# When the second MLP's weights are converted: two scopes of a one-core kernel cut 28 slots earlier, and the conversion's share of each slot set anew

## The chip, the core and the metric

One core of one Trainium2 chip runs the whole program. The metric is the device time of one launch in microseconds, as the median of three runs; a profiled execution of the same kernel has a time and a span of its own, given below.

## What is computed

Attention through 32 landmarks with a Newton inverse, then two mixers with an MLP behind each. All arrays are float32.

```python
B, H, S, D = 8, 8, 576, 64
x = (A @ Z @ C @ v)                                  # attention, then (B, S, 512)
h = x^T @ U @ V;  u = x + h^T                        # first mixer, rank 32
x = u + relu(u @ w_ch1) @ w_ch2                      # first MLP, 512 -> 2048 -> 512
mixed = real(fft(fft(x, axis=1), axis=2))            # second mixer
u = x + mixed
un = (u - mean(u)) / sqrt(var(u) + 1e-6)
out = u + relu(un @ w2_ch1) @ w2_ch2                 # second MLP
```

## The kernel before

**Numbers and weights.** Each float32 operand of a large product is split into a high and a low part, and three TensorE products stand for one. The weights come as 64-bit words. They are converted on the chip, once, into high and low parts of one tile of 128x1024 words: 512 KB come in, 512 KB go out to a scratch array `staged` (names `d` in the profile), from which the MLP loads them later. Such a conversion of one tile is a *staging*.

**Passes and slots.** Each MLP is run as two passes of 1024 hidden columns each: pass 0 and pass 1 of the first MLP, 2 and 3 of the second. A pass goes over chunks of 512 tokens (9 chunks in passes 0 and 1, 3 in passes 2 and 3). `Mlp.stream(p)` is a generator that a hand-written loop steps: one step is a *slot*, twelve 128x512 products on TensorE. A chunk is 16 slots: 8 that go up (L238 to L240, drained by a relu on ScalarE at L242 and a subtraction on VectorE at L243) and 8 that go down (L291 to L293, added at L302). The up products go through three PSUM banks in turn. Pass 0 takes chunk 0 in two halves, the second half last. At the end of a pass the weights of the next one are loaded (`w<-d` in the profile, L194), and residues and inputs of the next chunk are loaded beside them (L157, L146). All these transfers and those of the staging are issued by SyncE (SP) in the order of the code.

**Beside pass 0.** The attention of batch b runs in slots of the same loop (`slots.add`, `Batch.steps`); it ends, with the tail of the last batch, in slot 118 of 147 of that loop. The 16 tiles of pass 1 are staged there by `staging` (one generator step in every third slot, two in the others), 10 steps for a tile. Then the attention's pools are given back.

**Beside passes 1 to 3.** A second scope opens pools for the Fourier mixers. Mixer b (`Mixer.steps`) is spread over some 30 slots from `starts[b]`: folds, products over channels and tokens, unfolding, and the norm (`centre`, `sum_sq`, `sums_low` at L1250, `deviation`, whose product at L1255 waits for `sums_low`). The 32 tiles of passes 2 and 3 are staged by `staging_pairs`, and after them 28 sums of blocks of these weights by `staging_sums`. Both are one generator with prices, and `Pace.step(us)` lets it spend `us` in a slot: a tile costs 1.1 + 1.1 + 1.4 = 3.6. `room(s)` gives the slot's allowance. A tile has four parts: the split of the tile before it (ScalarE L50 and GpSimd L51 into the one buffer `stg`, which has to be stored before it is written again), then three pairs of VectorE instructions (L1379 with L1380; L1386 with L1388, and an absolute value on ScalarE at L1387; L1390 with L1391). What `Pace` has not done when the loop ends is done by `later.rest()` in one go.

**The last part.** `Mlp.pairs` runs the remaining six chunks of passes 2 and 3 as pairs by a seven-product scheme (L329 to L331). Its `prepare` loads normalised inputs (`acc<-un`, L146), splits them (ScalarE L389, VectorE L376), and its products start from banks that ScalarE copies (L406).

Of the kernel before, what the change touches and what calls it, by code (L numbers as in the profile page):

```python
# [28 lines left out]
HM = FF // P // 2  # L29
# [11 lines left out]
def body(ctx: ExitStack, tc: tile.TileContext, qT, kT, vn, mU, mV, w11, w12, w21, w22,  # L41
# [68 lines left out]
    def stage(cv, src, dst, bufs, raw=None):  # L110
        if raw is None:
            raw = cv.tile([P, 1024], U32, name="wraw", bufs=2)
        fetch_raw(raw, src)
        yield from wait(5)
        st = cv.tile([P, 2, 512], F32R, name="stg", bufs=1)
        yield from convert(cv, raw, st, bufs)
        yield from wait(1)
        nc.sync.dma_start(dst, f32(st))
# [1198 lines left out]
    def pool(name, **k):  # L1317
        return tc.tile_pool(name=name, bufs=1, reuse_waits="tile", **k)

    def chained(gens):  # L1320
        for g in gens:
            yield from g

    def some(gen, n):
        for _ in range(n):
            next(gen, 0)
# [21 lines left out]
    passes = [(U1, U1, ByChunk(y1), None), (U1, ByChunk(y1), X1, staged[1]),  # L1348
              (UN, None, ByChunk(y2), staged[2]), (UN, ByChunk(y2), ByChunk(y3), staged[3])]

    def staging(cv, p, bufs=1):
        return chained([stage(cv, srcs[p][i], staged[p][i], bufs) for i in range(2 * HM)])

    def staging_pairs(cv, passes):
        tiles = [(srcs[p][i], staged[p][i]) for p in passes for i in range(2 * HM)]
        raws = []

        def fetch():
            if len(raws) < len(tiles):
                raw = cv.tile([P, 1024], U32, name="wraw", bufs=2)  # L1360
                fetch_raw(raw, tiles[len(raws)][0])
                raws.append(raw)
                due["raw"] = clock[0] + 2

        fetch()
        former = None
        for i, (_, dst) in enumerate(tiles):
            yield from ready("raw")
            u = raws[i].rearrange("p (n two) -> p n two", two=2)
            lo, hi = u[:, :, 0], u[:, :, 1]  # L1370
            if former:
                st = cv.tile([P, 2, 512], F32R, name="stg", bufs=1)
                split(st[:, 0, :], st[:, 1, :], former[0], nc.gpsimd)
            fetch()
            yield 1.1
            a = cv.tile([P, 512], U32, name="cva", bufs=2)
            p = cv.tile([P, 512], U32, name="cvp", bufs=1)
            pf, af = f32(p), f32(a)
            nc.vector.tensor_scalar(a, hi, 3, 0x3FFFFFFF, op0=ALU.logical_shift_left, op1=ALU.bitwise_and)  # L1379
            nc.vector.scalar_tensor_tensor(out=a, in0=hi, scalar=0xC0000000, in1=a, op0=ALU.bitwise_and,  # L1380
                                           op1=ALU.bitwise_or)
            yield 0
            if former:
                nc.sync.dma_start(former[1], f32(st))
            yield 1.1
            nc.vector.tensor_scalar(p, a, 0xFF800000, None, op0=ALU.bitwise_and)  # L1386
            nc.scalar.activation(f32(hi), f32(hi), AF.Abs)  # L1387
            nc.vector.scalar_tensor_tensor(out=pf, in0=lo, scalar=2.0 ** -52, in1=pf, op0=ALU.mult, op1=ALU.mult)  # L1388
            yield 1.4
            nc.vector.tensor_tensor(pf, pf, af, op=ALU.add)  # L1390
            nc.vector.scalar_tensor_tensor(out=af, in0=f32(hi), scalar=MINNORM, in1=pf, op0=ALU.is_ge, op1=ALU.mult)  # L1391
            former = af, dst
            yield 0
        st = cv.tile([P, 2, 512], F32R, name="stg", bufs=1)
        split(st[:, 0, :], st[:, 1, :], former[0], nc.gpsimd)
        yield 0
        nc.sync.dma_start(former[1], f32(st))
# [85 lines left out]
    with pool("mm") as mp, pool("pm", space=PSUM) as pm:  # L1483
# [31 lines left out]
                old = new  # L1515
            yield from old

        EARLY = 8
        with pool("aa") as ap_, pool("ac") as ac, pool("cv0") as cv0, pool("pt", space=PSUM) as psb:
            t = {}  # L1520
            batches = [Batch(ap_, psb, t, b, mlp) for b in range(B)]
            slots = Slots()
            FIRST, GAP = -1 - Batch.LAST, 11
            half = (0, 1, 2, 4, 6, 8, 9, 10)
            for b in range(B):
                slots.add(GAP + STEPS * (b - 1) - 23 + 2 * (b == 1) if b else FIRST, batches[b].steps(batches[b + 1] if b + 1 < B else None))
            slots.add(GAP + STEPS * (B - 1) - 10, [(0, lambda: mlp.get_tail(B))])
            slots.add(GAP + STEPS * (B - 1) - 8, ((k, lambda k=k: mlp.hand_tail(B, k)) for k in range(4)))

            slots.add(FIRST, [(11, lambda: place_v(t))])  # L1530

            sums = {**{n - 11: [(1, 'k', 3 * n, 3 * n + 3)] for n in range(6)}, 3: [(2, 'k', 0, 6)], 5: [(2, 'k', 6, 12)], 7: [(2, 'k', 12, 18)]}

            def filler(s):

                if s in sums:
                    for b, nm, first, last in sums[s]:
                        batches[b].landmark_sums(nm, first, last)
                    return

                ps = mlp.bank()
                for _ in range(6):
                    nc.tensor.matmul(ps[:, 0:P], t["ident"], t["ident"], start=True, stop=True)

            with tc.manual_schedule():
                for what in "kq":
                    batches[0].load(what)
                attention_constants(ac, t)
                small, large = attention_setup(t, ap_, cv0), direct()
                some(small, 1)  # L1550
                some(large, 1)
                batches[0].load("v")
                some(large, 1)
                convs = chained([small, large])
                for s in range(FIRST, 0):
                    slots.run(s)
                    if s - FIRST in (6, *range(10, 20)):
                        filler(s)
                    some(convs, 0 if s < FIRST + 4 else 1 + s % 2)
                later, gen = staging(cv0, 1, 2), mlp.stream(0)  # L1560
                for s in range(N + GAP - 8):
                    if s >= GAP or s in half:
                        next(gen)
                    else:
                        filler(s)
                    slots.run(s)
                    if s < GAP + 13:
                        some(convs, 2)
                        if s == GAP + 12:
                            some(convs, 99)  # L1570
                    else:
                        some(later, 1 if s % 3 == 2 else 2)
                some(later, 999)
                some(gen, 9)
        with tc.manual_schedule():
            scales = Scales(rs)
            mlp.plan(UN, [(c, c + 1) for c in range(PLAIN, NCH, 2)], quarters)
            with pool("cv") as cv, pool("fp") as fp, pool("fc") as fc, pool("pf", space=PSUM) as psb:
                f = {}
                slots = Slots()  # L1580
                starts = (33, 58, 83, 108, 133, 157, 182, 206)
                for b, s in enumerate(starts):
                    slots.add(s, Mixer(fp, psb, f, b).steps(b + 1 == B))
                later = Pace(chained([staging_pairs(cv, (2, 3)), staging_sums(cv)]))
                gen = mlp.stream(1)
                setup = fourier_setup(f, fc, fp)

                def room(s):
                    r = s - max((a for a in starts if a <= s), default=-99)
                    return 1.45 if r > 40 else 1.4 if r in (*range(10, 21), 23, 24) else .7 if r in (4, 9, 21, 22) else 0  # L1590

                for s in range(N + 2 * PLAIN * STEPS - LEAD):
                    if s in (N, N + PLAIN * STEPS):
                        some(gen, 9)
                        gen = mlp.stream(2 + (s > N))
                    next(gen)
                    slots.run(s)
                    next(setup, 0)
                    later.step(room(s))
                later.rest()  # L1600
            assert not slots.at
            with pool("tl") as mlp.last_pool, pool("tp", space=PSUM) as mlp.last_ps:
                last = mlp.pairs(quarters, Y, scales, U2, ByChunk(y3))
                next(last)
                for s in range(LEAD):
                    next(gen)
                    next(last)
                    next(last)
                some(gen, 9)
                for _ in last:  # L1610
                    pass
# [83 lines left out]
```

## Time and profile before

| | us |
|---|---|
| median of 3 runs | 1787.58 (1785.87 to 1788.69) |
| the profiled execution | 1789.14 |
| its span in the profile | 1787.4 |
| TensorE busy in it | 1757.6 (98%) |
| VectorE busy | 1171.2 (66%) |
| ScalarE busy | 735.6 (41%) |
| GpSimd busy | 328.2 (18%) |

The span is what the trace covers; 1.7 us of the execution lie around it. In this trace pass 0's loop reaches slot 119 at about 495 us, pass 1 begins at 571, mixer 0's first slot is at 661, and the pairs begin at about 1305.

### The profile page before, as it was taken

Reading aid. Unit: us, or ns where it says so; the run is one execution under the profiler, and the core shown is the slowest. Engines: PE = TensorE matmul, PEld = TensorE weight load, DVE = VectorE, ACT = ScalarE, POOL = GpSimd, SP = SyncE. Lnnn points to the kernel's source line nnn. Section 1 sums busy time; section 2 is a strip of 40 time slices with the busy share of each in tenths; the row PEclk is TensorE's granted clock in tenths of the full one; section 3 lists DMA queues with packets and bytes.
Section 4 is the critical chain, followed back from the end, with each engine's and each line's share of the span. In section 5 each row is a group of like instructions: output and inputs, shape, how many; then the busy total and the mean of one; then the engine's idle time right before and its main releaser. Section 6 shows DMA issues by size and latency. Waiting matters only on the chain.

```text
span 1787.4 us, 30912 instructions
## 1 busy us (share of the span) xinstructions
PE 1757.6 (98%) x11905; PEld 1432.7 (80%) x11905; DVE 1171.2 (66%) x2028; ACT 735.6 (41%) x1520; POOL 328.2 (18%) x314
## 2 busy tenths in 40 slices
PE   6999999999999999999999999999999999999999
PEld 4777777777788888888878888888878888888887
DVE  7897666566322977888886665657575674577564
ACT  4554443444211333433342333434256445454642
POOL 3324211221110321211111122211111001100100
PEclk9999999999999999999999999999999999999999
DMA  7555456443536764546555954776688778878764
GB/s 254 182 174 171 152 175 206 155 162 105 179 137 249 242 234 154 183 164 216 179 179 193 329 200 148 273 281 201 222 290 273 216 243 257 261 228 247 223 214 153
DMA packets 215895, 371.00 MB, mean 208 GB/s; under 512 B 28970, under 2 KB 129930, under 8 KB 215748
## 3 DMA queue, kind: packets, MB, share of 16 engines
q1 hardware_dynamic: 211140, 359.59, 60.9%
q10 hardware_dynamic: 4608, 9.44, 1.4%
q8 instruction: 94, 1.54, 0.4%
q14 instruction: 53, 0.43, 0.1%
HBM read 262.18 MB, written 106.17 MB: 206 GB/s over the span
## 4 chain that ended last, share of the span: by engine, by line
PE 88%; DVE 7%; DMA 2%; ACT 1%; issue 1%; SPq 0%; POOL 0%; DVEq 0%; ACTq 0%
PE ps L291 9%; PE ps L293 9%; PE ps L292 9%; PE ps L238 9%; PE ps L240 8%; PE ps L239 8%; PE ps L329 7%; PE ps L331 7%; PE ps L330 7%; PE ps L554 1%; PE ps L553 1%; PE ps L555 1%; PE ps_f L77 1%; PE ps_f L76 1%; PE ps_f L75 1%
## 5 line engine op out<-in xcount | busy, mean ns | idle before, releaser
L238 PE MATMUL ps<-x,w 128*128 128x512 f32 x768 | 305.4, 398 | 0.2 <-DVE g L243 0.2
L291 PE MATMUL ps<-g,w 128*128 128x512 f32 x768 | 304.2, 396 | 0.0
L240 PE MATMUL ps<-x,w 128*128 128x512 f32 x768 | 299.8, 390 | 0.0
L293 PE MATMUL ps<-g,w 128*128 128x512 f32 x768 | 299.8, 390 | 0.0
L239 PE MATMUL ps<-x,w 128*128 128x512 f32 x768 | 299.4, 390 | 0.0
L292 PE MATMUL ps<-g,w 128*128 128x512 f32 x768 | 299.2, 390 | 0.0
L243 DVE SCALAR_TENSOR_TENSOR g<-ps,g 128x512 fp32r<-128x512 f32 x192 | 132.4, 690 | 206.7 <-ACT g L242 206.4
L242 ACT ACTIVATE g<-ps 128x512 fp32r<-128x512 f32 x192 | 114.0, 597 | 264.0 <-PE ps L240 263.4
L291 PEld LDWEIGHTS ps<-g,w 128*128 128x128 f32 x768 | 144.3, 188 | 31.9 <-issue 3.5
L240 PEld LDWEIGHTS ps<-x,w 128*128 128x128 f32 x768 | 144.1, 188 | 31.4
L293 PEld LDWEIGHTS ps<-g,w 128*128 128x128 f32 x768 | 144.1, 188 | 31.1
L238 PEld LDWEIGHTS ps<-x,w 128*128 128x128 f32 x768 | 144.3, 188 | 29.9 <-DVE g L243 0.6
L292 PEld LDWEIGHTS ps<-g,w 128*128 128x128 f32 x768 | 144.4, 188 | 27.4
L239 PEld LDWEIGHTS ps<-x,w 128*128 128x128 f32 x768 | 144.4, 188 | 26.9
L302 DVE TENSOR_TENSOR xf<-ps,xf 128x512 f32<-128x512 f32 x88 | 60.5, 687 | 86.7 <-PE ps L293 84.6
L406 ACT COPY ps<-ps 128x512 f32<-128x512 f32 x126 | 72.4, 575 | 94.4 <-PE ps L331 93.4
L51 POOL TENSOR_TENSOR stg<-cva,stg 128x512 fp32r<-128x512 f32 x48 | 65.4, 1363 | 216.8 <-ACT stg L50 190.4
L458 POOL TENSOR_TENSOR w<-w,w 128x512 f32<-128x512 f32 x24 | 33.3, 1389 | 362.1 <-DMA w<-rs 181.6
L329 PE MATMUL ps<-xs,w 128*128 128x512 f32 x240 | 94.2, 392 | 1.9 <-ACT ps L406 1.9
L331 PE MATMUL ps<-xs,w 128*128 128x512 f32 x240 | 94.1, 392 | 0.0
L330 PE MATMUL ps<-xs,w 128*128 128x512 f32 x240 | 93.9, 391 | 0.0
L51 POOL TENSOR_TENSOR x<-xf,x 128x512 fp32r<-128x512 f32 (+7 forms) x48 | 60.1, 1254 | 157.9 <-ACT x L50 122.7
(420 smaller groups left out, 3356.9 us busy)
## 6 DMA issues: line engine op xcount, KB each, us to landing
w<-e SPq DMA_DIRECT2D x84, 512.0 KB
w<-d SPq DMA_DIRECT2D x126, 256.0 KB
w<-d SPq DMA_DIRECT2D x60, 512.0 KB
wraw<-w SPq DMA_DIRECT2D x56, 512.0 KB
d<-stg SPq DMA_DIRECT2D x48, 512.0 KB
y<-xf SPq DMA_DIRECT2D x64, 256.0 KB
xf<-y SPq DMA_DIRECT2D x52, 256.0 KB
u<-u1T ACTq DMA_DIRECT2D x32, 288.0 KB
```

The lines of the kernel that those rows point to most:

```text
L51: (eng or nc.vector).tensor_tensor(lo, src, f32(hi), op=ALU.subtract)
L238: nc.tensor.matmul(ps, wh, xh, start=k == 0, stop=False)
L239: nc.tensor.matmul(ps, wl, xh, start=False, stop=False)
L240: nc.tensor.matmul(ps, wh, xl, start=False, stop=k == 3)
L242: nc.scalar.activation(g[:, 0, :], ps, AF.Relu)
L243: nc.vector.scalar_tensor_tensor(out=g[:, 1, :], in0=ps, scalar=0.0, in1=f32(g[:, 0, :]), op0=ALU.max, op1=ALU.subtract)
L291: nc.tensor.matmul(ps, wh, gh, start=k == m0, stop=False)
L292: nc.tensor.matmul(ps, wl, gh, start=False, stop=False)
L293: nc.tensor.matmul(ps, wh, gl, start=False, stop=k == m1 - 1)
L329: nc.tensor.matmul(ps, wh, xh, start=first and k == 0, stop=False, skip_group_check=True)
L330: nc.tensor.matmul(ps, wl, xh, start=False, stop=False, skip_group_check=True)
L331: nc.tensor.matmul(ps, wh, xl, start=False, stop=last and k == 1, skip_group_check=True)
```

## The change

The first scope ends with slot `end`, the last slot that holds a step of the attention plus one: 119, where it was 147. (The change's own words count 27 slots; the loop counts 28, slots 119 to 146.) `staging` stages 14 of the 16 tiles of pass 1. The two others go into `staging_pairs`, ahead of the 32 tiles of passes 2 and 3, and this generator starts in slot 119 of pass 0, in the new pools, with an allowance of 1.6 a slot. In pass 1 the allowance ahead of mixer 0 is 1.6 where it was 1.45; beside the mixers it stays 1.4 in 13 slots of each (r = 10 to 20, 23, 24), and the .7 in r = 4, 9, 21 and 22 is gone.

```diff
-    def staging(cv, p, bufs=1):
-        return chained([stage(cv, srcs[p][i], staged[p][i], bufs) for i in range(2 * HM)])
+    def staging(cv, n):
+        return chained([stage(cv, srcs[1][i], staged[1][i], 2) for i in range(n)])
-    def staging_pairs(cv, passes):
-        tiles = [(srcs[p][i], staged[p][i]) for p in passes for i in range(2 * HM)]
+    def staging_pairs(cv, first):
+        tiles = [(srcs[p][i], staged[p][i]) for p in range(1, 4) for i in range(2 * HM)][first:]
...
-        EARLY = 8
+        EARLY, ALONG = 8, 14
...
-                later, gen = staging(cv0, 1, 2), mlp.stream(0)
-                for s in range(N + GAP - 8):
+                later, gen = staging(cv0, ALONG), mlp.stream(0)
+                end = max(slots.at) + 1
+                for s in range(end):
...
                 some(later, 999)
-                some(gen, 9)
+                assert not slots.at
...
             with pool("cv") as cv, pool("fp") as fp, pool("fc") as fc, pool("pf", space=PSUM) as psb:
+                later = Pace(chained([staging_pairs(cv, ALONG), staging_sums(cv)]))
+                for s in range(end, N + GAP - 8):
+                    next(gen)
+                    later.step(1.6)
+                some(gen, 9)
...
-                later = Pace(chained([staging_pairs(cv, (2, 3)), staging_sums(cv)]))
...
-                    return 1.45 if r > 40 else 1.4 if r in (*range(10, 21), 23, 24) else .7 if r in (4, 9, 21, 22) else 0
+                    return 1.6 if r > 40 else 1.4 if r in (*range(10, 21), 23, 24) else 0
```

TensorE's products stand in the same order before and after. Three places show what moves on the others.

On SP, at the end of pass 0 (stores of `y` are the second half of chunk 0, `w<-d` are weights of pass 1, `wraw<-w` fetches a tile to be staged, `d<-stg` stores one). Before:

```order
L160 DMA y_0_75<-xf 128x512
L194 DMA w_6945<-d_8_114 128x1024
L194 DMA w_6947<-d_9_115 128x1024
L160 DMA y_0_75<-xf 128x512
L194 DMA w_6970<-d_10_116 128x1024
L194 DMA w_6972<-d_11_117 128x1024
L160 DMA y_0_75<-xf 128x512
```

and of the change:

```order
L160 DMA y_0_75<-xf 128x512
L194 DMA w_7082<-d_8_114 128x1024
L194 DMA w_7084<-d_9_115 128x1024
L87 DMA wraw<-w 128x1024
L160 DMA y_0_75<-xf 128x512
L194 DMA w_7116<-d_10_116 128x1024
L194 DMA w_7118<-d_11_117 128x1024
L1384 DMA d_7_129<-stg 128x1024
L160 DMA y_0_75<-xf 128x512
```

A fetch and a store of 512 KB have come between the weights that pass 1 loads.

On VectorE, in the norm of mixer 0, ahead of the subtraction into `le` on which L1255 waits. Before:

```order
L1390 TENSOR_TENSOR cvp<-cvp,cva 128x512
L1391 SCALAR_TENSOR_TENSOR cva<-wraw,cvp 128x512
L51 TENSOR_TENSOR x<-xf,x 128x512
L1250 TENSOR_TENSOR ho<-cc,ho 128x288
L1379 TENSOR_SCALAR cva<-wraw 128x512
L1380 SCALAR_TENSOR_TENSOR cva<-wraw,cva 128x512
L302 TENSOR_TENSOR xf<-ps,xf 128x512
L1265 TENSOR_TENSOR Z<-U,ps_l 128x1152
L1386 TENSOR_SCALAR cvp<-cva 128x512
L1388 SCALAR_TENSOR_TENSOR cvp<-wraw,cvp 128x512
L51 TENSOR_TENSOR x<-xf,x 128x512
```

and of the change:

```order
L51 TENSOR_TENSOR x<-xf,x 128x512
L1250 TENSOR_TENSOR ho<-cc,ho 128x288
L1379 TENSOR_SCALAR cva<-wraw 128x512
L1380 SCALAR_TENSOR_TENSOR cva<-wraw,cva 128x512
L302 TENSOR_TENSOR xf<-ps,xf 128x512
L1265 TENSOR_TENSOR Z<-U,ps_l 128x1152
L1386 TENSOR_SCALAR cvp<-cva 128x512
L1388 SCALAR_TENSOR_TENSOR cvp<-wraw,cvp 128x512
L1390 TENSOR_TENSOR cvp<-cvp,cva 128x512
L1391 SCALAR_TENSOR_TENSOR cva<-wraw,cvp 128x512
L51 TENSOR_TENSOR x<-xf,x 128x512
```

The pair L1390 and L1391 has gone from the front of this stretch to its end; the count of staging instructions in it is the same six.

On SP, at the entry of the pairs, ahead of the first `acc<-un` (`rs<-r` stores the last mixer's scale, `e` are sums of blocks). Before:

```order
L1293 DMA rs_205<-r 128x288
L1441 DMA e_2_180<-cva 128x512
L1441 DMA e_2_180<-wraw 128x512
L1441 DMA e_1_179<-stg 128x512 x2
L1441 DMA e_3_181<-cva 128x512
L1441 DMA e_3_181<-blk 128x512
L146 DMA acc<-un_193 128x256
```

and of the change:

```order
L192 DMA w_13722<-d_0_122 128x2x256
L192 DMA w_13722<-d_1_123 128x2x256
L1293 DMA rs_205<-r 128x288
L146 DMA acc<-un_193 128x256
L146 DMA acc<-un_194 128x256
```

The six stores of the last sums no longer stand between the last mixer and the loads of the pairs.

## Rows read from the trace of the kernel before

**Rows 1.** The page: its span, and each engine's busy time and instructions.

```profile
span 1787.4 us, 30912 instructions
...
PE 1757.6 (98%) x11905; PEld 1432.7 (80%) x11905; DVE 1171.2 (66%) x2028; ACT 735.6 (41%) x1520; POOL 328.2 (18%) x314
```

**Rows 2.** TensorE's waits from 495 us to the end.

```profile
PE ps_l L1255 <- DVE le L1250: 2.7, 3, 1.4
PE ps L329 <- ACT ps L406: 1.9, 1, 1.9
PE ps_f L1202 <- DVE Z L51: 0.6, 1, 0.6
PE ps L238 <- DVE g L243: 0.2, 1, 0.2
```

**Rows 3.** TensorE's timeline at the entry of the pairs: start, length, instruction.

```profile
1321.31 0.50 PE L329 MATMUL ps<-xs,w 128*128 128x512 f32 x1 [1.88 <-ACT ps L406]
...
1322.58 0.61 PE L331 MATMUL ps<-xs,w 128*128 128x512 f32 x1
...
1325.97 0.41 PE L330 MATMUL ps<-xs,w 128*128 128x512 f32 x1
```

**Rows 4.** ScalarE's timeline at the same place.

```profile
1309.56 0.62 ACT L50 CAST cva<-blk 128x512 fp32r<-128x512 f32 x1 [4.33 <-DMA e<-cva]
...
1320.16 0.62 ACT L389 CAST xs<-acc 128x512 fp32r<-128x512 f32 x1 [1.83 <-DMA acc<-un]
1320.68 1.06 ACT L406 COPY ps<-ps 128x512 f32<-128x512 f32 x2
```

**Rows 5.** SP's timeline of issues at the same place.

```profile
1304.92 0.60 SPq L1293 DMA_DIRECT2D rs<-r  x1
...
1311.98 3.73 SPq L146 DMA_DIRECT2D acc<-un  x8
```

**Rows 6.** Stretches: us, busy PE, PEld, DVE, ACT, POOL, clock, DMA share, GB/s.

```profile
549.00:571.00 22.00, 22.00 (x99) 18.22 (x98) 7.31 (x11) 4.46 (x8) 2.63 (x2) 1.00 0.86 299
571.00:593.00 22.00, 22.00 (x99) 18.22 (x98) 14.75 (x23) 8.22 (x14) 2.87 (x3) 1.00 1.00 358
593.00:661.00 68.00, 68.00 (x302) 56.31 (x301) 59.13 (x82) 23.04 (x41) 23.59 (x20) 1.00 0.61 212
1319.00:1326.00 7.00, 5.12 (x16) 3.74 (x16) 5.50 (x9) 5.38 (x11) 0.00 (x0) 0.76 1.04 376
```

**Rows 7.** VectorE's groups by line, 571 to 661 us: busy, mean ns, idle before.

```profile
L1380 DVE SCALAR_TENSOR_TENSOR cva<-wraw,cva 128x512 uint32<-128x512 uint32 x13 | 11.9, 918 | 0.4
L243 DVE SCALAR_TENSOR_TENSOR g<-ps,g 128x512 fp32r<-128x512 f32 x16 | 11.0, 688 | 11.6 <-ACT g L242 11.6
L1386 DVE TENSOR_SCALAR cvp<-cva 128x512 uint32<-128x512 uint32 x12 | 10.5, 872 | 0.1
L1390 DVE TENSOR_TENSOR cvp<-cvp,cva 128x512 f32<-128x512 f32 x12 | 9.3, 779 | 0.2
L1388 DVE SCALAR_TENSOR_TENSOR cvp<-wraw,cvp 128x512 f32<-128x512 uint32 x12 | 8.4, 701 | 0.4
L1391 DVE SCALAR_TENSOR_TENSOR cva<-wraw,cvp 128x512 f32<-128x512 f32 x12 | 8.3, 692 | 1.4 <-DVE cvp L1390 0.5
L1379 DVE TENSOR_SCALAR cva<-wraw 128x512 uint32<-128x512 uint32 x13 | 7.5, 574 | 0.0
```

**Rows 8.** ScalarE's longest wait, 571 to 661 us: total, times, longest.

```profile
ACT stg L50 <- DMA d<-stg: 24.7, 9, 5.1
```

**Rows 9.** VectorE's timeline in pass 1 ahead of the mixers.

```profile
624.26 0.42 DVE L1379 TENSOR_SCALAR cva<-wraw 128x512 uint32<-128x512 uint32 x1
...
629.43 0.69 DVE L243 SCALAR_TENSOR_TENSOR g<-ps,g 128x512 fp32r<-128x512 f32 x1 [4.02 <-ACT g L242]
```

**Rows 10.** VectorE's timeline in the norm of mixer 0.

```profile
740.39 1.52 DVE L1379 TENSOR_SCALAR cva<-wraw 128x512 uint32<-128x512 uint32 x1
...
750.09 0.88 DVE L1250 TENSOR_TENSOR le<-cc,le 128x288 fp32r<-128x288 f32 x1
```

**Rows 11.** GpSimd's timeline there.

```profile
740.28 1.35 POOL L51 TENSOR_TENSOR stg<-cva,stg 128x512 fp32r<-128x512 f32 x1 [8.67 <-ACT stg L50]
```

## The prediction

> **What bounds the kernel now.** I read the page first: TensorE is busy 98% of the span, 1757.6 of 1787.4 us [rows 1], and the change leaves its products and their order alone. So only its idle time and its clock can move. TensorE's waits come next, from the place where the change begins (495 us) to the end: they are few, 1.9 + 2.7 + 0.6 + 0.2 = 5.4 us [rows 2]. Earlier waits lie in the attention's start, which is the same in both kernels up to slot 100 or so. The reader should see two kinds. The norm's product L1255 waits three times for VectorE, 2.7 us, the longest 1.4 [rows 2]: in mixers 0 and 2, beside conversions, and a little in mixer 7. And the first product of the pairs that needs a copied bank waits 1.88 us for ScalarE's L406 [rows 3]. Behind that wait the clock is low: the granted share from 1319 to 1326 us is 0.76 [rows 6], and from 1322.58 to 1325.97 eight products start 0.42 us apart, 3.39 us in all [rows 3], where at full rate 68 us hold some 300, 0.227 each [rows 6], or twelve to a slot of 2.72. That is 3.39 - 8 x 0.227 = 1.6 us more at 1.2 GHz instead of 2.4.
>
> The Trainium skill says of this ("TensorE: Matmul & The Clock Gate", What's actually happening) that the throttled state is the default and activity releases it; the trace agrees as far as a drop behind this wait goes. By the waits alone the entry of the pairs is worth 1.9 us, with the clock 3.5; the sum takes the clock in because the rows show it.
>
> **What the change does, step by step.** *The entry of the pairs.* Following `Pace` through the allowances, the kernel before ends its last tile in slot 121 of the loop over passes 1 to 3 and begins the sums in 123; after the last slot, 235, one addition and two subtractions with their splits are left, and `rest()` issues them at once, in front of `prepare`. The rows show the price. ScalarE stands 4.33 us in front of a split until the store of `e` has landed [rows 4]; the six stores stand on SP between 1304.92 and the first `acc<-un` at 1311.98 [rows 5]; the last of these loads lands so late that ScalarE waits 1.83 us for it, and L406 stands behind that wait [rows 4]. In the change 12 tiles are done when pass 1 begins, 26 when mixer 0 begins, all 34 by slot 75, and the sums end in slot 207. Nothing is left for `rest()`. The loads can be issued right behind the store of 1304.92, some 6 us sooner, which is more than the 1.88 us that TensorE waits. So I take both the wait and the slow clock as gone: 1.9 + 1.6 = 3.5 us (bounds 0, if something else is late at the same place, and 3.5).
>
> *The norms.* Mixers 2 and 7 lose most of the staging beside their norm: mixer 2 has three sums' instructions there where it had ten of the conversion's, mixer 7 none. Their share is 2.7 - 1.4 = 1.3 us [rows 2]; I take it whole. Mixer 0 keeps six instructions of a conversion in the stretch that ends with `le` (the order of VectorE shows it), so fewer allowances alone do not free it. But one thing moves: the split of the tile before was issued in the same slot as L1379, and is now two slots ahead. In the kernel before GpSimd's split starts at 740.28 [rows 11] and L1379 beside it takes 1.52 us [rows 10], where the same instruction with GpSimd idle takes 0.42 [rows 9]: 1.1 us. I take 1.1 of the 1.4 (bounds 0 and 1.4). Of the 0.6 and the 0.2 [rows 2], which lie beside staging in mixers 3 and 4, where the sums are now differently placed but as dense, I take half: 0.4 (0 to 0.8).
>
> Together 3.5 + 1.3 + 1.1 + 0.4 = 6.3 us, at most 7.0.
>
> *What is added.* The conversions now run through the end of pass 0 and the start of pass 1. VectorE and ScalarE have room there: from 549 to 571 VectorE is busy 7.31 us of 22 [rows 6]. The transfers have less. That stretch and the next, in which pass 1's weights come in, move 299 and 358 GB/s, at shares of 0.86 and 1.00 [rows 6]: 22 x 0.299 + 22 x 0.358 = 14.5 MB. A tile adds 2 x 0.52 = 1.05 MB. At 1.6 a slot it takes 3.6 / 1.6 = 2.25 slots, 6.1 us, so 44 us hold 7.2 tiles, 7.5 MB, less some 2 MB that the kernel before converts there itself: 20 MB. The fastest stretch I find moves 376 GB/s [rows 6]: 16.5 MB in 44 us. So about 3.5 MB, 9 us of transfer, are late at 593 us, and then work off, since the stretch behind moves only 212 GB/s [rows 6].
>
> The Trainium skill puts the limit of the sixteen engines' ports at some 436 GB/s ("SBUF — State Buffer", A bandwidth-pool intuition that's wrong). By that figure, as an estimate, 19.2 MB would pass and only 2 us be late. No row here reaches it, so the rows' 9 us stand.
>
> What is late first is the store `d<-stg`, because the single `stg` makes ScalarE wait for it, and the relu L242 of the next bank stands behind on ScalarE. That wait is there already ahead of the mixers: 24.7 us in 9 times, 2.7 each, the longest 5.1 [rows 8]. TensorE was not held even by that one: VectorE stood 4.02 us in front of L243 [rows 9], but with three banks a slot's result need only be taken within two further slots, 5.4 us, of which the relu and the subtraction with their gaps need about 1.4. So some 4 us of lateness cost nothing. In the change each wait grows by the shorter interval, (2.48 - 2.25) x 2.72 = 0.6 us, and near 571 to 593 by a share of the 9 us, 2.3 for each of four tiles: 2.7 + 0.6 + 2.3 = 5.6, or 1.6 over what is free. Three of these tiles meet up slots, so at most 4.8 us; if the burst spreads over more tiles or over the down half, 0. I take 1.8, near the lower part, since the rows show no wait of TensorE there at full share. At the place of the longest wait 5.1 + 0.6 may cost another 0 to 0.7, in which I see 0.1.
>
> The opening of the pools costs nothing that I can find: the attention's last use of them is its tail, some slots ahead, and the first fetch into the new pool stands on SP where the kernel before had one too. Its bound is a wait of one fetch on VectorE in a down half, hidden behind three banks.
>
> **Sum.** 6.3 - 1.9 = 4.4 us less. Against the profiled execution of 1789.14 (span 1787.4 and 1.7 around it) that is 1784.7; the median of the runs lies 1.6 lower, 1787.58, and so the forecast is 1783.2 us.
>
> **Rivals.** *The burst takes the gain back.* Seven tiles at the upper 1.6 us each and the 0.7 at the later place are 12 us; half of that, 5 us, leaves 6.3 - 5 = 1.3 us, 1786.3, no measurable change (0.2% is 3.6 us, about what a measurement of this kernel can tell). For it speaks the share of 1.00 [rows 6], against it that the waits before are absorbed.
>
> *The waits only move.* The norm of mixer 0 and the places at mixers 3 and 4 stay, because six instructions are six wherever they stand, and only the entry of the pairs and mixers 2 and 7 gain: 4.8 - 1.9 = 2.9 us, 1784.7.
>
> *The pairs' entry does not gain.* If `prepare`'s VectorE chain and not the loads is what is late, the 3.5 us stay: 2.8 - 1.9 = 0.9 us, 1786.7. Against it speaks ScalarE's own wait for `acc<-un` directly in front of L406 [rows 4].
>
> *Slower: VectorE is the bound of the up slots.* A tile's six VectorE instructions take 918 + 872 + 779 + 701 + 692 + 574 = 4.54 us [rows 7]; over 2.25 slots that is 2.02 a slot, and with L243's 0.69 [rows 7] 2.71 of 2.72. At 2.48 slots it was 2.52. If the faster pace lets GpSimd's splits meet more of them, a slot may need more than it has. One split more per tile, 1.1 us, makes 0.49 a slot, 3.9 us over the eight up slots of a chunk, which the free 4 us still take. It decides when the excess exceeds 0.5 us a slot; at 1.0 it costs 4 us in each of the three chunks converted before mixer 0 that were not so dense, 12 us: 6.3 - 12, slower by 5.7, 1793.3. The down slots between let VectorE catch up, which speaks against it.
>
> The Trainium skill has the rule behind this rival ("SBUF — State Buffer", Who interferes with whom): the port pair that VectorE and GpSimd share is an exclusive lock, and the loser waits out the whole instruction. By that rule 1.3 us is the price of a meeting; the trace agrees with 1.1.
>
> **Chances.** The forecast (4 to 7 us less) 0.58; the burst takes it back 0.17; waits only move 0.09; no gain at the entry 0.08; slower 0.08, in which I count a burst over 10 us too. The range holds eight in ten from the full gain without a cost, 1787.6 - 7.0 less a little for the runs' own spread, to no change at all: 1779.8 to 1787.6. Faster by over 0.2%: 0.58; within 0.2%: 0.34; slower: 0.08.
>
> **What would show it.** Right: no wait of L329 on L406 at the entry and a granted clock of 1.00 there; `acc<-un` issued within 1 us of the last `rs` store; no wait at L1255 in mixers 2 and 7, under 0.4 us in mixer 0. Wrong: waits of TensorE on L243 between 571 and 600 us of more than 4 us in all, with ScalarE's waits for `d<-stg` well over 5 us; VectorE busy over 95% in the up slots there; or a wait of L329 that stays with the loads already landed.

## The result and the profile after

The changed kernel takes 1799.95 us (1799.55 to 1800.92, 4 runs) against 1786.72 (1785.21 to 1788.69, 4 runs): a ratio of 1.0074, 95% interval 1.0057 to 1.0092. It is slower by 13 us, where I forecast 1783.2 and gave "slower" a chance of 0.08. The two profiled spans differ by less, 1797.8 - 1787.4 = 10.4 us, since the execution of the kernel before that was profiled (1789.14) is one of its longer ones, and that of the changed kernel (1799.55) its shortest. The account below is of these 10.4 us.

TensorE's waits from 495 us to the end, in the changed kernel (total, times, longest), answer to [rows 2]:

```profile
PE ps L238 <- DVE g L243: 5.4, 4, 3.9
PE ps L238 <- DVE xf L302: 2.9, 3, 1.9
PE ps L291 <- DVE g L243: 1.1, 1, 1.1
PE ps_l L1255 <- DVE le L1250: 0.9, 1, 0.9
PE ps L293 <- DVE g L243: 0.5, 1, 0.5
```

The wait of L329 for L406 is gone and the norms wait less. In their place stand waits for a bank that VectorE has not yet drained. Three stretches of the kernel before, then the same three of the one after with 571 to 593 us ahead of them (columns as in [rows 6]), show where:

```profile
560.00:615.00 55.00, 55.00 (x244) 45.54 (x243) 40.44 (x55) 19.04 (x33) 15.61 (x12) 1.00 0.79 278
615.00:1300.00 685.00, 681.58 (x3340) 571.87 (x3339) 486.46 (x781) 248.44 (x484) 137.86 (x114) 1.00 0.62 211
1300.00:1345.00 45.00, 42.99 (x181) 34.77 (x180) 33.62 (x54) 24.73 (x47) 8.08 (x7) 0.96 0.91 313
```

```profile
571.00:593.00 22.00, 16.38 (x60) 11.96 (x60) 9.85 (x16) 2.16 (x4) 1.79 (x3) 0.92 1.03 404
560.00:615.00 55.00, 46.85 (x181) 36.23 (x180) 34.82 (x53) 16.99 (x30) 12.85 (x11) 0.91 0.89 334
615.00:1300.00 685.00, 682.22 (x3336) 571.35 (x3335) 455.49 (x729) 236.30 (x463) 134.49 (x111) 1.00 0.60 200
1300.00:1345.00 45.00, 45.00 (x203) 37.36 (x202) 29.84 (x48) 24.04 (x44) 4.54 (x4) 1.00 0.75 244
```

TensorE's products stand in the same order in both kernels, and both traces hold all 11905, so one product can be found in both by its place. Four of them, at 560 us, at the end of the first chunk of pass 1, in the last mixer's norm and behind the entry of the pairs, in the kernel before and then in the changed one:

```profile
559.80 0.39 PE L291 MATMUL ps<-g,w 128*128 128x512 f32 x1
614.20 0.39 PE L238 MATMUL ps<-x,w 128*128 128x512 f32 x1
1299.28 0.43 PE L1255 MATMUL ps_l<-lo,ones 128*128 128x288 f32 x2
1327.15 0.40 PE L329 MATMUL ps<-xs,w 128*128 128x512 f32 x1
```

```profile
559.85 0.39 PE L291 MATMUL ps<-g,w 128*128 128x512 f32 x1
628.63 0.39 PE L238 MATMUL ps<-x,w 128*128 128x512 f32 x1
1313.92 0.43 PE L1255 MATMUL ps_l<-lo,ones 128*128 128x288 f32 x2
1337.57 0.39 PE L329 MATMUL ps<-xs,w 128*128 128x512 f32 x1
```

The changed kernel is 0.05, 14.43, 14.64 and 10.42 us late at them. So 14.4 us are lost between the first two; from there to the last mixer's norm 0.2 are lost, although idle time falls by 3.4 - 2.8 = 0.6 there; and 4.2 are given back from that norm to behind the entry, of which the entry's wait and clock are some 3.8. The sum is 10.4 us, the difference of the spans.

From 560 to 615 us all products have one size, so their count tells nearly the same without a second trace: the kernel before does 244, the changed kernel 181, and 63 x 0.227 = 14.3 us. Of the 14.4 us, 8.15 are idle time; some 4.0 are the low clock, 20 products about 0.43 us apart where they should be 0.227 (seven from 580.68 on, thirteen from 595.50 on). The rest lies beside the waits: idle time is counted from the modelled end of a product, so a wait sets the products back by a little more than it shows.

What ScalarE waits for from 560 to 615 us in the changed kernel:

```profile
ACT stg L50 <- DMA d<-stg: 27.7, 5, 12.7
ACT tabh L50 <- DMA big<-tabs: 4.6, 1, 4.6
ACT x L50 <- DMA xf<-u: 3.3, 1, 3.3
```

And the longest of these waits, with the store it is for, on SP, on ScalarE, and behind it on VectorE and TensorE:

```profile
572.82 0.32 SPq L1384 DMA_DIRECT2D d<-stg  x1
```

```profile
582.77 0.62 ACT L50 CAST stg<-cva 128x512 fp32r<-128x512 f32 x1 [12.74 <-DMA d<-stg]
583.29 0.67 ACT L1387 ACTIVATE wraw<-wraw 128x512 f32<-128x512 f32 x1
583.86 1.07 ACT L242 ACTIVATE g<-ps 128x512 fp32r<-128x512 f32 x2
```

```profile
584.47 0.69 DVE L243 SCALAR_TENSOR_TENSOR g<-ps,g 128x512 fp32r<-128x512 f32 x1 [3.89 <-ACT g L242]
```

```profile
585.22 0.50 PE L238 MATMUL ps<-x,w 128*128 128x512 f32 x1 [1.04 <-DVE g L243]
```

One store of 512 KB is issued at 572.82 and has landed by 582.77, 10 us later. ScalarE stands in front of the buffer all that time, and two relus that had been ready run behind it in one piece. Of the 12.7 us of this wait, 2.8 passed before SP issued the store. The second such wait, 8.1 us, holds TensorE for 3.94, and the products that follow start at the lower clock:

```profile
590.58 0.39 PE L240 MATMUL ps<-x,w 128*128 128x512 f32 x1
594.91 0.79 PE L238 MATMUL ps<-x,w 128*128 128x512 f32 x1 [3.94 <-DVE g L243]
595.50 0.63 PE L239 MATMUL ps<-x,w 128*128 128x512 f32 x1
595.92 0.63 PE L240 MATMUL ps<-x,w 128*128 128x512 f32 x1
596.35 0.63 PE L238 MATMUL ps<-x,w 128*128 128x512 f32 x1
```

The store is not the only late transfer here. A raw tile that SP issued at 567.82 has landed by 577.77, also 10 us later. VectorE stands 3.15 us in front of it; behind that wait stands the addition L302, and TensorE waits 1.89 us for its bank. The first seven slow products follow this wait. A smaller one, 0.63 us at 574.67, has no late transfer before it: VectorE was busy with conversions ahead of the same addition.

```profile
567.82 0.38 SPq L87 DMA_DIRECT2D wraw<-w  x1
```

```profile
577.77 0.43 DVE L1379 TENSOR_SCALAR cva<-wraw 128x512 uint32<-128x512 uint32 x1 [3.15 <-DMA wraw<-w]
```

```profile
579.57 0.50 PE L238 MATMUL ps<-x,w 128*128 128x512 f32 x1 [1.89 <-DVE xf L302]
```

### The profile page after: what moved, and what is told of

It is laid out like the page before. It is cut to its first block, busy times and chain, and to the rows that moved or that the text cites. A ratio compares the mean times of both kernels' runs of the same rounds, so it can differ in the third digit from the quotient of the medians.

```text
span 1797.8 us, 30920 instructions
## 1 busy us (share of the span) xinstructions
PE 1763.4 (98%) x11905; PEld 1434.0 (80%) x11905; DVE 1172.2 (65%) x2030; ACT 735.9 (41%) x1520; POOL 327.0 (18%) x312
## 4 chain that ended last, share of the span: by engine, by line
PE 84%; DVE 6%; DMA 6%; ACT 1%; issue 1%; POOL 1%; SPq 0%; ACTq 0%; DVEq 0%; POOLq 0%
PE ps L291 8%; PE ps L293 8%; PE ps L292 8%; PE ps L238 8%; PE ps L240 8%; PE ps L239 8%; PE ps L330 7%; PE ps L331 7%; PE ps L329 7%; DMA d<-stg 3%; PE ps L554 1%; PE ps L553 1%; PE ps L555 1%; PE ps_f L76 1%; PE ps_f L77 1%
## 5 line engine op out<-in xcount | busy, mean ns | idle before, releaser
L243 DVE SCALAR_TENSOR_TENSOR g<-ps,g 128x512 fp32r<-128x512 f32 x192 | 132.2, 689 | 212.1 <-ACT g L242 211.0
L406 ACT COPY ps<-ps 128x512 f32<-128x512 f32 x126 | 72.4, 575 | 95.5 <-PE ps L331 94.4
L302 DVE TENSOR_TENSOR xf<-ps,xf 128x512 f32<-128x512 f32 x88 | 60.4, 687 | 76.8 <-PE ps L293 75.4
L329 PE MATMUL ps<-xs,w 128*128 128x512 f32 x240 | 93.4, 389 | 0.0
```

Source lines behind the costliest of these rows:

```text
L243: nc.vector.scalar_tensor_tensor(out=g[:, 1, :], in0=ps, scalar=0.0, in1=f32(g[:, 0, :]), op0=ALU.max, op1=ALU.subtract)
L329: nc.tensor.matmul(ps, wh, xh, start=first and k == 0, stop=False, skip_group_check=True)
```

## The experiments

Theory A was that the store of the converted tile, queued behind the weights of pass 1, is the whole cost; B that 1.6 a slot is too fast for VectorE; C that opening the pools sooner costs; D that weights and inputs of pass 1 are themselves late. Each kernel is judged by the products it does from 560 to 615 us, against the 244 of the kernel before at 0.227 us each, since what it does at the entry of the pairs depends on how many sums are left over. Where no range stands beside a time, it is that of one execution, and only the count is used.

**No conversion in the last ten slots of pass 0** (the changed kernel, and 1.45 ahead of mixer 0):

```diff
                     next(gen)
-                    later.step(1.6)
+                    if s < end + 18:
+                        later.step(1.6)
...
-                    return 1.6 if r > 40 else 1.4 if r in (*range(10, 21), 23, 24) else 0
+                    return 1.45 if r > 40 else 1.4 if r in (*range(10, 21), 23, 24) else 0
```

Expected: 

> The changed kernel with no conversion in the last ten slots of pass 0, in which the weights of pass 1 come in, and with the allowance of 1.45 ahead of the mixers as in the kernel before. Theory A (what costs the time is the store of a converted tile, queued behind the weights of pass 1; ScalarE waits for it because of the single buffer, and the relus stand behind): TensorE's waits between 560 and 610 us fall from 9 us and a low clock to under 1 us at full clock; the sums still end before the pairs, so the entry stays free; about 1783 us, 16 to 17 below the changed kernel. Theory B (the conversions are too fast for VectorE wherever they meet up slots): the eight up slots of chunk 8 show waits too, and the loss shrinks by no more than half, to about 1793. Theory C (pools given back sooner cost by themselves): no better than 1797.

Measured: 1783.37 us (1781.24 to 1784.56), ratio 0.9977 (0.9967 to 0.9986). The stretch has 239 products and one wait of 1.0 us, which ends at 594. 18 slots of chunk 7 and 8 convert at 1.6 without a wait of TensorE, so B and C fall as the main cause; with ten slots less conversion the loss is 1.1 us.

```profile
560.00:615.00 55.00, 53.97 (x239) 44.37 (x238) 38.03 (x53) 17.91 (x32) 14.70 (x12) 1.00 0.81 292
```

**Only the last ten slots convert:**

```diff
-                    later.step(1.6)
+                    if s >= end + 18:
+                        later.step(1.6)
```

Expected: 

> The mirror of the pause: of the 28 early slots of the changed kernel only the last ten of pass 0 convert, at 1.6, and the 18 ahead of them do not. Theory A: the loss between 560 and 610 us stays nearly whole, TensorE idle 6 us or more and the clock at its lower level behind it, ScalarE waiting over 8 us at once for a store; 1796 to 1802 us. Theory B: the loss follows the number of slots, a third of it is left, 1788 to 1791 us.

Measured: 1805.66 us. 190 products: (244 - 190) x 0.227 = 12.3 us of the 14.4 lost, from a third of the slots. The place decides. That it is slower than the changed kernel comes from the entry of the pairs, where many sums are left over again: TensorE waits 7.5 us there.

```profile
560.00:615.00 55.00, 45.66 (x190) 36.52 (x189) 37.55 (x55) 17.12 (x30) 13.24 (x11) 0.94 0.88 327
1300.00:1345.00 45.00, 37.20 (x157) 30.05 (x156) 31.89 (x49) 20.86 (x39) 8.84 (x7) 0.92 0.83 279
```

**1.45 instead of 1.6, nothing else:** in pass 0 and ahead of mixer 0.

```diff
-                    later.step(1.6)
+                    later.step(1.45)
...
-                    return 1.6 if r > 40 else 1.4 if r in (*range(10, 21), 23, 24) else 0
+                    return 1.45 if r > 40 else 1.4 if r in (*range(10, 21), 23, 24) else 0
```

Expected: 

> The changed kernel with 1.45 where it has 1.6, in pass 0 and ahead of the mixers. Theory E: the burst at the end of pass 0 is a tenth smaller and meets the weights all the same; the loss between 560 and 615 us stays above 7 us of the 14; 1791 to 1798 us. Theory B (VectorE cannot keep the pace of 1.6): 1.45 ran without a wait in the kernel before, so the loss falls under 2 us; 1783 to 1786 us.

(E, the theory named here, comes up below, with the transfers alone; this kernel was run after them.)

Measured: 1798.79 us, 177 products, 15.2 us lost. The pace is not it in this stretch. Behind it the waits differ: from 616 us to the entry TensorE has a single one, of 1.2 us at 653, and mixer 0's wait at L1255 is gone.

**A second buffer for the converted tile** (every other tile, up to the 24th, goes into a part of the mixers' `U`, which is not in use yet):

```diff
-                st = cv.tile([P, 2, 512], F32R, name="stg", bufs=1)
+                st = spare if i % 2 and i < 24 else cv.tile([P, 2, 512], F32R, name="stg", bufs=1)
...
```

Expected: 

> The changed kernel with a second buffer for the converted tile, lent from a mixer's tile that is not in use yet, in turn with the first up to the 24th tile. Nothing else moves: the same transfers at the same places. Theory A: ScalarE's waits for the store fall from 68 us between 495 and 700 us to under 25, the longest from 12.7 to under 6, and TensorE's idle time between 560 and 610 us from 9 us to under 4; 1785 to 1790 us. Theory D (the port of the transfers itself is what is late: weights, inputs and raw tiles): the waits move to VectorE's instructions on raw tiles and to TensorE's on weights, and the loss stays above two thirds, 1794 or more.

Measured: 1796.89 us, 189 products, 12.5 us lost. The waits for the store fall to 2.3 us, as A wants, and the loss hardly moves: A as I had put it falls. Other waits have taken the place, for a table of the Fourier mixers and for raw tiles:

```profile
ACT tabh L50 <- DMA big<-tabs: 11.8, 3, 9.0
ACT wraw L1387 <- DVE cva L1380: 6.3, 3, 3.8
DVE cva L1379 <- DMA wraw<-w: 7.9, 3, 3.8
```

**The transfers alone,** in the kernel before: no result is added, nothing waits for them.

```diff
...
+                    if s >= 119 and (s - 119) * 4 % 9 < 4:
+                        raw = cv0.tile([P, 1024], U32, name="wraw", bufs=2)
+                        fetch_raw(raw, srcs[2][len(extra)])
+                        for n in range(2):
+                            nc.sync.dma_start(void[len(extra)][:, n, :], kept)
+                        extra.append(s)
```

Expected: 

> The kernel before with the transfers alone: in slots 119 to 146 thirteen times a fetch of 512 KB and two stores of 256 KB that nothing waits for, and no conversion. It adds no result. Theory A: ScalarE waits for no store, so TensorE loses at most 2 us between 560 and 610 us although the queue is as full as in the changed kernel; 1787 to 1790 us. Theory D: the loss is there without any conversion, 6 us or more, 1793 or more.

Measured: 1798.49 us, 200 products, 10.0 us lost without a conversion at the end of pass 0. That looks like D, but TensorE waits for no weight. It waits for one drain, 7.1 us, and ScalarE shows why:

```profile
ACT tabh L50 <- DMA big<-tabs: 9.9, 1, 9.9
```

In the kernel before, that first table had been fetched long ahead; SP issues it 70 us before pass 1, with the store of the last tile of pass 1:

```profile
501.30 0.38 SPq L118 DMA_DIRECT2D d<-stg  x1
501.77 0.41 SPq L1066 DMA_DIRECT2D big<-tabs  x1
```

With the edit SP issues it behind the weights:

```profile
582.20 0.33 SPq L1066 DMA_DIRECT2D big<-tabs  x1
```

So this kernel differs from the one before in more than the transfers: the edit has moved the table's fetch by 80 us too, and the 10.0 us are the cost of both together.

So a new theory, E: the port is full in any of these kernels, and what costs the time is that an engine that works in order stands in front of whichever late transfer it needs, with drains of banks behind it. By this theory it does not matter whether that is a store, a table or a raw tile.

**The transfers alone, with the tables set up from slot 12 of pass 1:**

```diff
-                    next(setup, 0)
+                    if s >= 12:
+                        next(setup, 0)
```

Expected: 

> The kernel with the bare transfers, in which ScalarE stood 9.9 us in front of the first table of the Fourier mixers, with the setup of these tables begun in slot 12 of pass 1 where it was slot 0. The transfers at the end of pass 0 are as many as before. Theory E (the port is full, and what costs the time is that ScalarE, in order, stands in front of whichever late transfer it needs, with relus behind it): nothing on ScalarE needs a late transfer in the first slots of pass 1 any more, so TensorE's loss between 560 and 610 us falls from 9.7 us with the clock to under 2; about 1788 to 1790 us. Theory D (weights and inputs of pass 1 are themselves late): the loss stays, over 6 us, with waits for DMA on TensorE; 1795 or more.

Measured: 1795.87 us, 216 products: 6.4 us are still lost, more than I expected. The wait has moved to VectorE:

```profile
DVE cva L1379 <- DMA wraw<-w: 9.0, 1, 9.0
```

**The second buffer, with the tables from slot 12** (the edit of the second buffer and the one just shown):

Expected: 

> The changed kernel with the second buffer for the converted tile and the tables' setup from slot 12. Theory E: the store and the tables are both off ScalarE's way; what stays is the absolute value of a tile whose raw words come late. The loss between 560 and 610 us falls from 12 us with the clock to under 5; 1784 to 1790 us. Theory D: it stays at 10 or more, 1796.

Measured: 1792.77 us, 203 products, 9.3 us lost where I expected under 5. VectorE's L1379 waits 12.8 us in four times for raw tiles.

**The transfers alone, with tables and conversions from slot 12** (the tables' edit, and):

```diff
-                    return 1.45 if r > 40 else 1.4 if r in (*range(10, 21), 23, 24) else .7 if r in (4, 9, 21, 22) else 0
+                    return (1.45 if s >= 12 else 0) if r > 40 else 1.4 if r in (*range(10, 21), 23, 24) else .7 if r in (4, 9, 21, 22) else 0
```

Expected: 

> The bare transfers and the tables from slot 12, and no conversion before slot 12 of pass 1 either, since VectorE stood 9.0 us in front of a raw tile there. Theory E, widened to both in-order engines (ScalarE and VectorE lose the time in front of whichever late transfer they need, and drains of banks stand behind): nothing of this kind is left in the first slots, so TensorE loses under 1 us between 560 and 615 us, at full clock, although the stretch from 571 to 593 us moves over 380 GB/s. Theory D (weights or inputs late by themselves): 4 us or more stay. The time as a whole says little, because more sums are left for the entry of the pairs.

Measured: 244 products, nothing lost, with the port from 571 to 593 us as full as in the changed kernel (behind these 22 us it is emptier here):

```profile
571.00:593.00 22.00, 22.00 (x99) 18.22 (x98) 5.53 (x8) 4.19 (x7) 0.00 (x0) 1.00 1.04 406
560.00:615.00 55.00, 55.00 (x244) 45.53 (x244) 18.80 (x29) 12.36 (x20) 6.70 (x6) 1.00 0.74 282
```

This separates D from E. Over these 22 us 406 GB/s and a share of 1.04 cost TensorE nothing, as no in-order engine needs a late transfer. The kernel before has such a stretch of its own, later and likewise without a wait of TensorE:

```profile
1153.00:1175.00 22.00, 22.00 (x115) 18.46 (x114) 13.37 (x22) 6.96 (x14) 2.82 (x2) 1.00 1.03 411
```

(The time, 1796.17, is that of the entry: 7.2 us of wait for the left-over sums.)

**The pause, with the tables from slot 12** (the first experiment's edit and the tables'):

Expected: 

> The kernel with the pause in the last ten slots of pass 0, with the tables' setup from slot 12 as well. Its one wait near 592 us, 1.0 us, stands behind a store that lands 6.6 us late. Theory E: taking the tables' 1.2 MB from between the weights lets the store land sooner, the wait goes, 1 us less than the pause alone: 1781 to 1783 us. Rival: the tables were not in the way there; no difference, or the setup collides with the conversions of chunk 1 and costs 1 to 2 us.

Measured: 1780.99 us (1780.21 to 1782.10, 6 runs), ratio 0.9966 (0.9953 to 0.9978). From 495 us to the end TensorE has one wait left. It is the fastest version, 0.34% under the kernel before.

```profile
PE ps_l L1255 <- DVE le L1250: 0.3, 1, 0.3
```

**The entry of the pairs by itself** (the kernel before, denser staging beside the later mixers):

```diff
+                    if s >= 108 and r in (4, 9, 21, 22):
+                        return 1.4
```

Expected: 

> The kernel before with an allowance of 1.4 where it was 0.7 beside the mixers from slot 108 on, so that the sums end in slot 224 and nothing is left for the rest in front of the pairs. It isolates the entry of the pairs. My step: the wait of L329 for L406 and the low clock behind it go, 3.5 us less, if the denser staging costs the norms nothing: 1783 to 1785 us, with a clock of 1.00 at the entry. Rival: something else at the entry is late by as much, and the wait stays; 1787, or more if the norms of mixers 3 to 7 now wait.

Measured: 1794.63 us (1792.94 to 1796.09), ratio 1.0043 (1.0028 to 1.0058). The entry is free, with a clock of 1.00, but the mixers lose more than it gives: TensorE stands idle 9.2 of the 685 us from 615 to 1300, where it was 3.4. The largest wait is 4.0 us, and it has the same cause, a store of `stg`, at the place where the kernel before is fullest (its row from 1153 to 1175 above):

```profile
615.00:1300.00 685.00, 675.78 (x3298) 566.12 (x3298) 489.58 (x775) 244.15 (x477) 142.87 (x115) 1.00 0.62 212
1300.00:1345.00 45.00, 45.00 (x202) 37.28 (x201) 32.32 (x53) 25.34 (x47) 4.22 (x4) 1.00 0.80 265
```

```profile
1178.91 0.62 ACT L50 CAST stg<-wraw 128x512 fp32r<-128x512 f32 x1 [7.83 <-DMA e<-stg]
```

## Why the prediction was wrong

**The entry of the pairs** was right in mechanism and size: 3.5 us forecast, 3.8 measured. In the changed kernel `acc<-un` is issued at 1320.17, right behind the last store of `rs` at 1319.55, where 7 us lay between them [rows 5]; L406 waits only for TensorE, and the clock is 1.00.

**The norms** and small waits were to give 2.8 us, and up to the last norm nothing came of it on balance. The old waits did shrink, by about what was forecast: mixers 2 and 7 gained as put, the small waits of mixers 3 and 4 went whole. Mixer 0 kept 0.9 us of its wait, where I had taken off 1.1 of 1.4 for GpSimd's split moving away: L1379 does take 0.41 there now, but the pair L1390 and L1391 has come in behind it. But new waits of 1.1, 0.3, 0.3 and 0.2 us behind 615 us, for L243 and L302, set the products back by as much. With 1.45 instead of 1.6 mixer 0's wait and all of these were gone, and one of 1.2 us at 653 had come; what makes each of them late was not tried by itself. In the fastest version this stretch is idle for 0.3 us only (684.72 of 685), so the gain was to be had.

**The term that failed is the burst**, 1.8 us with bounds 0 and 4.8, against 14.4 measured. The sign of being wrong that the prediction names came up: 5.0 us of waits on L243 up to 600 us, with waits of 12.7 and 8.1 for the store. That the port would be over-full was right: 404 GB/s at a share of 1.03 was seen. The step that failed is the next: "2.3 for each of four tiles", the 9 us spread evenly, so that each wait came just over what three banks hide. The lateness was not shared out. The raw tile issued at 567.82 and the store issued at 572.82 took 10 us each, and the next store, which ScalarE waited 8.1 us for, took 8: each of them was late by about the whole backlog, not by a quarter of it. Three more things were left out. The clock: I priced it at the entry and not here, where it is some 4.0 of the 14.4 us. The other transfers: I followed the store only, but in the changed kernel a raw tile already holds TensorE for 1.89 us, and the second buffer showed that a table and the raw tiles stand ready to take the store's place. And the evidence that I leaned on, that the kernel before has no wait of TensorE at a share of 1.00 [rows 6], did not show a tolerance. Its first table, as its rows on SP above show, was fetched before the burst, and it converted nothing between the last tile of pass 1 and slot 0; bare transfers, with that table among them, cost it 10 us in the same place.

The rival "the burst takes the gain back" had the place and the mechanism, and a price of 5 us (half of its 12 us would be 6); its upper price of 12 was near what came. The rival of VectorE as the bound was wrong as the main cause: the slots of chunk 8 ran at 1.6 without a wait in the changed kernel and with the pause, and 1.45 did not help. It accounts for at most the 0.63 us at 574.67 and what little TensorE lost just ahead of it.

The rate was read too low: I took 376 GB/s from a stretch of 7 us [rows 6], and the trace of the kernel before has 411 over 22 us, in the row above from 1153 to 1175. By that, as an estimate, 44 us pass 18.1 MB, and of the forecast's 20 MB 1.9 MB, some 5 us, are late and not 9. With it the term would have come out smaller still, so it is not this that failed. The Trainium skill's limit of some 436 GB/s ("SBUF — State Buffer", A bandwidth-pool intuition that's wrong) was not reached in any stretch shown here.

Open is how much of the loss each single transfer carries: with the second buffer and the late tables 9.3 us stayed, and the raw tiles' waits there were seen but not taken away by themselves. Not tried either is whether the transfers are late by the port alone or also by their order on one queue, by issuing some of them elsewhere.

## What to carry to other kernels

When work is moved into a stretch where the transfers are already near their limit, it is not enough to ask whether the engines have room: list what each in-order engine will wait for there (a buffer's store, a table, a raw tile) and what stands behind it, and price each such wait at the whole backlog and not at a share of it, with the clock behind it. Here, removing one such wait let the next late transfer take its place, and keeping every dependent instruction out of the stretch took the loss away at a full port. A "no wait before" is evidence only if the same dependent instructions stood there before.

## What the runs showed of the chip

TensorE's clock fell to its lower level behind waits of 1.88 us (the entry before; eight products 0.42 us apart), 1.89 us (the raw tile in the changed kernel; seven) and 3.94 us (thirteen). It stayed at 2.4 GHz behind the norms' single waits of 1.4 us, and behind one of 1.84 us in the second buffer with late tables. The Trainium skill ("TensorE: Matmul & The Clock Gate", What's actually happening) gives the two levels of 1.2 and 2.4 GHz, and the products' spacing of 0.42 to 0.43 against 0.227 us agrees with them. In a full queue one 512 KB store took 10 us to land, among transfers of 404 GB/s, and so did one 512 KB fetch.
